# A fused attention and rational feed-forward kernel: the engines' order written by hand, elementwise work in one piece a block, K turned by DMA

## The chip, the cores and the metric

One core of one Trainium2 chip. The metric is device time in microseconds (us) of one execution; lower is better. The kernel before has a median of 319.29 us (315.65 to 320.66, 4 runs). Medians and ranges in this document are over all runs; ratios use the fast ones alone (a run more than 1.5% above the fastest of its kernel counts as slow, as 320.66 does).

The engines go by short names: PE multiplies matrices, DVE (VectorE), ACT (ScalarE) and POOL (GpSimd) work element by element; SP and POOL also issue DMA transfers (copies to and from the chip's memories), which land some us later. SBUF is the on-chip memory, PSUM the banks into which PE writes. To "turn" is to transpose; the "spread" copies the turned K into the layout that the scores need.

## The reference, cut to what matters

```python
# attention: 4 batches, 8 heads, 768 positions, head dimension 64
scores = q @ k.T / sqrt(64)
keep   = (column < 4) | ((row - column >= 0) & (row - column < 128))   # 4 sinks and a window of 128
a      = softmax(where(keep, scores, -1e9));   x = a @ v               # x: 3072 x 512
# feed-forward: 512 -> 2048 -> 512, the activation is a quotient of two polynomials
h = x @ w_in
P = a0 + a1*h + a2*h**2 + a3*h**3
Q = 1 + |b0|*|h| + |b1|*h**2
out = (P / (Q + 1e-6)) @ w_out                                          # float32
```

The 3072 tokens are worked in 12 blocks of 256 (three to a batch). A block is 256 tokens times 2048 features; on chip that is 128 partitions times 4096 elements.

## The kernel before: the parts that matter

Both kernels divide h by |b0|/|b1| so that Q needs no coefficients: x or w_in is multiplied by one scalar, `csc`. The quotient is num * exp(-ln(Q)): DVE does the polynomial in bf16, ACT the logarithm and the exponential. The elementwise functions work on **half** a block:

```python
UC = NFFC // 2;  UW = UC * TS                      # 2048 elements a partition: half a block
# ... cut ...
def load_w_in(half):                               # w_in scaled on its way to bf16
    for c in range(NDMC):
        nc.sync.dma_start(out=t_f, in_=moe_w_in[...])
        nc.vector.tensor_scalar(out=w_in_sb[c][:, f0:f1], in0=t_f, scalar1=csc, scalar2=None, op0=ALU.mult)
# ... cut ...
def turn_k(s):                                     # K: 8 transposes on PE, then spread out of PSUM
    ps = ps_mp.tile([P, 512], FP32, tag="ps_m", name="ps_kT").bitcast(BF16)
    for t in range(NTS):
        for i in range(NPB):
            nc.tensor.transpose(ps[:, i, t * P:(t + 1) * P], kb[:, t, i * P:(i + 1) * P], ident)
    for e in range(2):
        nc.vector.tensor_copy(out=kT[lo:hi, :, lo:hi], in_=ps[lo:hi]...)
# ... cut: scores, exps, mask, attend ...
        nc.vector.tensor_tensor(out=dst, in0=o4[...], in1=rec[...], op=ALU.mult)      # x normalised
# ... cut ...
def even(i):       nc.vector.tensor_scalar(out=num[i], in0=sq[i], scalar1=a2, scalar2=a0, ...)
def odd(i):        nc.vector.tensor_scalar(out=sq[i], in0=sq[i], scalar1=a3, scalar2=a1, ...)
def odd_h(i):      nc.vector.tensor_tensor(out=sq[i], in0=sq[i], in1=hb[i], op=ALU.mult)
def numerator(i):  nc.vector.tensor_tensor(out=num[i], in0=num[i], in1=sq[i], op=ALU.add)
def gate(i):       nc.vector.tensor_tensor(out=g_of[m, u], in0=num[i], in1=den[i], op=ALU.mult)
# ... cut ...
for i in range(-3, NU + 4):                        # one half block a turn; scores three half blocks ahead
    # scores(i + 3), attend(i + 2), project_in(i), elementwise(i, i - 1), project_out(i - 3)
```

The program order of this loop is only a proposal: the framework's scheduler decides in which order each engine gets its instructions.

The softmax here doesn't subtract the row's maximum and nothing guards it: scores larger than these inputs give would overflow.

## Time and profile before

| | before |
|---|---|
| median us | 319.29 |
| first 256-token block at w_in (first `ps_h` matmul) | 44.31 us |
| third block at w_in (the milestone of the prediction) | 102.25 us |
| pace from the fourth block's `even` to the eighth's | 20.52 us a block |
| DVE busy, 200 to 220 us | 19.30 of 20 us |

The milestone is the first product that needs the second half of the third block's x; a few matmuls on its first half come before (at 92.20 us here). The pace is read from the starts of the DVE operation `even` (of its first half here): 136.81 us in the fourth block and 218.89 in the eighth. These four blocks have the whole list of work in every kernel; behind them the spreads of K run out, in some kernels one block earlier than in others. (The prediction took 19.85 from later blocks and another row; by `even` these, from 198.78 to 278.22 us, give 19.86.)

### The profile page before, as it was taken

The numbers are of one execution on the slowest core, as the hardware profiler recorded it, in microseconds if no ns is written. First come the engines' busy times: TensorE is split into PE (matmuls) and PEld (weight loads), VectorE is DVE, ScalarE is ACT, GpSimd is POOL, SyncE is SP. The second block draws the span as 40 slices with busy tenths as digits, with TensorE's granted clock in tenths as the row PEclk, the third lists the DMA queues.
The fourth block names the chain that finished last, engine by engine and source line by source line (L and its number), as shares of the span: only waits on it lengthen the run. The fifth ranks groups of instructions, "written<-read, shape, count | busy, mean of one in ns | idle before, by whom it ended". The sixth has DMA issues, their size and how long they took to land.

```text
span 318.6 us, 5033 instructions
## 1 busy us (share of the span) xinstructions
PE 240.5 (75%) x1920; PEld 167.4 (53%) x1920; DVE 250.4 (79%) x384; ACT 212.8 (67%) x194; POOL 127.1 (40%) x192
## 2 busy tenths in 40 slices
PE   0025448749348969998879989989899898979964
PEld 0014336638224746666647665577575675746521
DVE  7534520769936897899998999999999899897990
ACT  1013014657823993996878978889799897877951
POOL 9986667996884341534540113356200000000000
PEclk9999556979858998999999999999999999999999
DMA  4999999999999996996960627549510111110011
GB/s 132 111 209 192 204 184 151 99 131 103 111 107 136 102 123 84 86 82 86 107 76 17 76 54 56 72 58 107 72 44 22 36 51 49 35 33 33 35 66 66
DMA packets 110775, 28.67 MB, mean 90 GB/s; under 512 B 104608, under 2 KB 106656, under 8 KB 110752
## 3 DMA queue, kind: packets, MB, share of 16 engines
q0 software_dynamic: 78976, 11.56, 58.1%
q1 hardware_dynamic: 31776, 16.79, 23.6%
q8 instruction: 15, 0.25, 0.3%
q14 instruction: 8, 0.07, 0.1%
HBM read 27.30 MB, written 6.29 MB: 105 GB/s over the span
## 4 chain that ended last, share of the span: by engine, by line
DVE 33%; ACT 21%; DMA 19%; PE 10%; issue 7%; POOL 5%; SPq 3%; DVEq 0%; ACTq 0%; POOLq 0%
DMA xblk<-x_n 12%; ACT lnq L379 7%; ACT den L383 6%; DVE den L358 5%; DVE g L388 5%; PE ps_h L339 5%; DVE num L373 4%; DVE sq L370 4%; PE ps_out L398 3%; ACT e L274 3%; SPq L324 3%; DVE den L354 3%; ACT hb L342 3%; DVE num L362 2%; DMA q_bf<-in_q_dram 2%
## 5 line engine op out<-in xcount | busy, mean ns | idle before, releaser
L339 PE MATMUL ps_h<-xblk,w_in_sb 128*128 128x256 bf16 x768 | 98.0, 278 | 30.7 <-DMA xblk<-x_n 30.6
L339 PEld LDWEIGHTS <-w_in_sb 128*128 128x128 bf16 x768 | 74.4, 100 | 45.6 <-DMA xblk<-x_n 28.1
L398 PE MATMUL ps_out<-w_out_sb,g 128*128 128x512 bf16 x384 | 93.5, 391 | 3.7 <-DVE g L388 3.4
L97 POOL DMA_DIRECT2D v_bd<-in_v_dram x96 | 61.8, 663 | 55.4 <-PE ps_o L305 47.3
L274 ACT ACTIVATE e<-ps_s 128x768 bf16<-128x768 f32 x48 | 38.7, 806 | 53.2 <-PE ps_s L270 53.2
L342 ACT ACTIVATE hb<-ps_h 128x1024 bf16<-128x1024 f32 x48 | 48.7, 1018 | 21.1 <-PE ps_h L339 21.1
L398 PEld LDWEIGHTS <-g 128*128 128x128 bf16 x384 | 37.3, 101 | 44.0 <-issue 5.1
L379 ACT ACTIVATE lnq<-den,one_eps,qsc 128x2048 f32<-128x2048 bf16 x24 | 50.2, 2092 | 5.5 <-DVE den L358 5.5
L383 ACT ACTIVATE den<-lnq 128x2048 bf16<-128x2048 f32 x24 | 45.8, 1908 | 0.0
L270 PE MATMUL ps_s<-qT,kT 128*128 128x192 bf16 x192 | 27.4, 272 | 9.4 <-DVE kT L237 7.3
L305 PE MATMUL ps_o<-v_bd,e 128*128 128x130 bf16 x352 | 31.4, 226 | 3.0 <-DMA v_bd<-in_v_dram 1.8
L388 DVE TENSOR_TENSOR g<-num,den 128x2048 bf16<-128x2048 bf16 x24 | 29.4, 1223 | 5.4 <-ACT den L383 5.3
L358 DVE TENSOR_TENSOR den<-den,sq 128x2048 bf16<-128x2048 bf16 x24 | 29.4, 1223 | 2.5 <-ACT sq L348 2.0
L281 DVE TENSOR_TENSOR e<-e,edge 128x1024 bf16<-128x1024 bf16 x24 | 16.2, 675 | 17.7 <-ACT e L274 17.7
L373 DVE TENSOR_TENSOR num<-num,sq 128x2048 bf16<-128x2048 bf16 x24 | 29.3, 1222 | 0.4
L370 DVE TENSOR_TENSOR sq<-sq,hb 128x2048 bf16<-128x2048 bf16 x24 | 29.1, 1214 | 0.1
L305 PEld LDWEIGHTS <-e 128*128 128x128 bf16 x352 | 26.1, 101 | 5.2 <-issue 3.5
L88 POOL DMA_DIRECT2D k_bf<-in_k_dram x24 | 22.2, 931 | 15.9 <-PE ps_kT L232 14.9
L80 POOL DMA_DIRECT2D q_bf<-in_q_dram x24 | 21.7, 906 | 17.2 <-DMA qT<-q_bf 17.2
L270 PEld LDWEIGHTS <-kT 128*128 128x128 bf16 x192 | 18.0, 108 | 16.4 <-DVE kT L237 9.8
L348 ACT ACTIVATE sq<-hb 128x2048 bf16<-128x2048 bf16 x12 | 22.9, 1911 | 0.3
L232 PE MATMUL ps_kT<-ident,k_bf 128*128 128x128 bf16 x96 | 8.1, 233 | 19.9 <-POOL ident masks.py:199 18.9
(56 smaller groups left out, 224.1 us busy)
## 6 DMA issues: line engine op xcount, KB each, us to landing
out_dram<-o_t SPq DMA_DIRECT2D x24, 256.0 KB, 2.1
w_in_f<-in_moe_w_in_dram SPq DMA_DIRECT2D x8, 512.0 KB, 5.8
q_bf<-in_q_dram POOLq DMA_DIRECT2D x24, 128.0 KB, 4.8
k_bf<-in_k_dram POOLq DMA_DIRECT2D x24, 128.0 KB, 4.8
v_bd<-in_v_dram POOLq DMA_DIRECT2D x96, 32.0 KB, 3.8
w_out_sb<-in_moe_w_out_dram POOLq DMA_DIRECT2D x16, 128.0 KB, 6.7
xblk<-x_n SPq DMA_TRANSPOSE x48, 2.5
qT<-q_bf SPq DMA_TRANSPOSE x24, 4.0
```

The source lines that it names most:

```text
L97: nc.gpsimd.dma_start(out=t_[e * 64:(e + 1) * 64, i, :, e, 0:D], in_=v[b, h, g * TS:(g + 1) * TS, :].rearrange("(j p) d -> p j d", p=64))
L270: nc.tensor.matmul(ps[:, n // 2, (n % 2) * 192:(n % 2) * 192 + 192], lhsT=kT_fix[s % 2][:, i * NHF + n, :], rhs=qT_fix[b % 2][:, i, c:c + ...
L274: nc.scalar.activation(out=data.rearrange("p (a n) c -> p a n c", a=2), in_=ps[:, :, 0:384].rearrange("p a (n c) -> p a n c", n=2), func=A ...
L305: nc.tensor.matmul(ps_o[:, n, :], lhsT=l_, rhs=r_.rearrange("p e c -> p (e c)"), start=(m == 0), stop=(m == len(terms) - 1))
L339: nc.tensor.matmul(ps_h[:, n, :], lhsT=w_in_sb[c][:, fc * P:(fc + 1) * P], rhs=xblk[m][:, c, :], start=(c == 0), stop=(c == NDMC - 1))
L342: nc.scalar.activation(out=hb[i][:, half * w:(half + 1) * w], in_=ps_h.rearrange("p n c -> p (n c)"), func=AF.Copy)
L358: nc.vector.tensor_tensor(out=den[i], in0=den[i], in1=sq[i], op=ALU.add)
L373: nc.vector.tensor_tensor(out=num[i], in0=num[i], in1=sq[i], op=ALU.add)
L379: nc.scalar.activation(out=lnq[i], in_=den[i], func=AF.Ln, scale=qsc, bias=one_eps)
L383: nc.scalar.activation(out=den[i], in_=lnq[i], func=AF.Exp, scale=-1.0)
L388: nc.vector.tensor_tensor(out=g_of[m, u], in0=num[i], in1=den[i], op=ALU.mult)
L398: nc.tensor.matmul(ps_out[m, tt], lhsT=g_of[m, u][:, co:co + P], rhs=w_out_sb[fc], start=(fc == 0), stop=(fc == NFFC - 1))
```

## The change

The intent: keep DVE, the bound, without holes and give it less to do. `manual_schedule` turns the scheduler off, so that every engine works in program order; the loop goes over quarter blocks ("slots"), with the scores two blocks (eight slots) ahead of their block's w_in product, and w_out ten slots behind. Five elementwise kinds take a whole block at once (4096 wide). K is turned by DMA transposes on SP from the third block on. The first loads go raw through SP, and the first two blocks' K, Q and x are turned on PE. The scalar `csc` moves from w_in to the normalisation of x. PSUM changes too: a pool of two banks shared by four users becomes one bank for scores of sinks and attention, and one for w_out.

The diff has 938 lines; this is its core, with cuts marked:

```diff
+    ctx.enter_context(tc.manual_schedule())
...
-    ps_mp = ctx.enter_context(tc.tile_pool(name="ps_m", bufs=2, space=bass.MemoryType.PSUM))
+    ps_mp = ctx.enter_context(tc.tile_pool(name="ps_m", bufs=1, space=bass.MemoryType.PSUM))
+    ps_op = ctx.enter_context(tc.tile_pool(name="ps_o", bufs=1, space=bass.MemoryType.PSUM))
...
+    load_k(0)                                     # raw, on SP
+    for n in range(NQ_HW):
+        load_q(n)
+    load_v(0)
     nc.sync.dma_start(out=b_bc, in_=moe_b.partition_broadcast(P))
...
+        kT_flat[s] = a_kv.tile([P, NPB, TS], BF16, tag="kT_flat", name="kT_flat", bufs=3)
+        for t in range(NTS):
+            nc.sync.dma_start_transpose(out=kT_flat[s][:, :, t * P:(t + 1) * P], in_=kb[:, t, :])
...
-        nc.vector.tensor_tensor(
+        nc.vector.scalar_tensor_tensor(
+            out=dst, in0=o4[:, :, 0:D].rearrange("p (n e) c -> p n e c", e=2), scalar=csc,
...
+    ahead_s = {0: (), 1: (4, 5), 2: (6, 7), 3: (), 4: (8, 9), 5: (10, 11), 6: (12, 13),
+               7: (14, 15)}
+    ahead_a = {0: (), 1: (), 2: (4, 5), 3: (6, 7), 4: (), 5: (8, 9), 6: (10, 11), 7: (12, 13)}
+    spread_at = {4: 2, 6: 3, 7: 4}
+    turn_at = {0: 2, 2: 3, 4: 4, 6: 5}
+    for t in range(NSLOT + 14):
+        p, j = divmod(t, 4)
+        ns = ahead_s.get(t, (t + 8,))             # scores of this slot
+        na = ahead_a.get(t, (t + 6,))             # attends of this slot
...
+        if s < NSTEP:
+            turn_qk(s)
+            if s != 3:
+                feed(s + 2)
+        if t in (4, 5):
+            load_w_out(t - 4)
+        if t == 5:
+            feed(5)
...
+            if in_g:
+                gate(c - 1)                       # 4096 wide, as even, odd, odd_h, numerator
```

## The prediction

> **What bounds the kernel now.** I read the page first: the DVE row and the DMA row of its slices.
>
> ```profile
> PE 240.5 (75%) x1920; PEld 167.4 (53%) x1920; DVE 250.4 (79%) x384; ACT 212.8 (67%) x194; POOL 127.1 (40%) x192
> DVE  7534520769936897899998999999999899897990
> DMA  4999999999999996996960627549510111110011
> ```
>
> No engine is full on average, but the average mixes two stages: until about 110 us the DMA is full and DVE is not; after it, DVE is at 9 and the DMA falls away. The table of busy time by stretch, for one early and one late stretch, gives both (columns: stretch, its length, then busy us with counts of PE, weight load, DVE, ACT, POOL; clock, DMA share, GB/s):
>
> ```profile
> 80.00:100.00 20.00, 9.94 (x63) 5.55 (x60) 12.56 (x23) 9.65 (x10) 16.45 (x23) 0.66 1.86 110
> 200.00:220.00 20.00, 18.62 (x164) 13.35 (x162) 19.30 (x31) 17.69 (x17) 9.47 (x14) 1.00 0.66 64
> ```
>
> Late, DVE is busy 19.3 of 20 us: it is the bound. Early, every compute engine waits. The chain of waits says for what:
>
> ```profile
> 86.41 5.75 DMA xblk<-x_n
> 92.20 1.03 PE ps_h L339 x4
> 98.10 4.10 DMA xblk<-x_n
> 102.25 1.72 PE ps_h L339 x14
> 310.98 3.64 PE ps_out L398 x16
> ```
>
> The turned x block is asked for one half step before its use, and under the load of the early DMA it takes 4 to 7 us to land. The third 256-token block reaches w_in at 102.25 us; I use that point as a milestone. The ACT timeline gives the late pace, one lnq per half block:
>
> ```profile
> 198.92 2.08 ACT L379 ACTIVATE lnq<-den,one_eps,qsc 128x2048 f32<-128x2048 bf16 x1
> 278.34 2.10 ACT L379 ACTIVATE lnq<-den,one_eps,qsc 128x2048 f32<-128x2048 bf16 x1 [0.81 <-DVE den L358]
> ```
>
> Eight half blocks in 79.4 us: **19.85 us a block**, 12 blocks in all. So the time is 102 us to the milestone, then 216 us for ten blocks and the drain.
>
> **What the Trainium skill says.** (1) "VectorE: DVE Perf Modes", section "Side-by-side: where the cycles go for N=2048 bf16": 2048 elements cost about 1224 ns at two per cycle, of which some 150 cycles are fixed. The trace agrees for the two-input operations (1223, below), so a 4096-wide one is estimated at (2048+150)/0.96 = 2.29 us. The one-input ones read 0.82 here, not the page's 0.69 (they carry two per-partition scalars); I keep the trace's fixed part, 0.82 - 0.53 = 0.29, and estimate 1.07 + 0.29 = 1.36 us at 4096. (2) The same page, "Why PSUM operands drop a tier": a copy out of PSUM cannot run four per cycle. The K spread out of PSUM takes 684 ns for 1024 elements; out of SBUF I estimate (256+150)/0.96 = 0.42 us. (3) "TensorE: Matmul & The Clock Gate", section "Wait — 56ns, not 53.3ns?": a warm matmul starts every N/2.4 + 2.5 ns; sixteen of 512 then take 3.45 us, and the chain's last line has 3.64 with the end of the last, which agrees. (4) "DMA: Bandwidth & Descriptors", section "Issuing engines are not separate DMA queues": loads moved to another issuer still share the 16 engines. The early stretch, with both queues in use and xblk slow, agrees.
>
> ```profile
> L358 DVE TENSOR_TENSOR den<-den,sq 128x2048 bf16<-128x2048 bf16 x24 | 29.4, 1223 | 2.5 <-ACT sq L348 2.0
> L362 DVE TENSOR_SCALAR num<-sq,acoef 128x2048 bf16<-128x2048 bf16 x24 | 19.6, 815 | 0.1
> L237 DVE COPY kT<-ps_kT 64x1024 bf16<-64x1024 bf16 x24 | 16.4, 684 | 0.2
> L313 DVE TENSOR_TENSOR x_n<-ps_o,rec 128x256 bf16<-128x256 f32 x48 | 20.0, 418 | 0.1
> ```
>
> **The change part by part, in the steady stage, per block.** Neighbouring DVE operations overlap by about 0.09 us in the timeline, so I count from start to start.
> - Five of nine elementwise kinds go from 2x2048 to 1x4096. Three two-input ones: 6 x 1.17 = 7.0 becomes 3 x 2.25 = 6.75. Two one-input ones: 4 x 0.84 = 3.4 becomes 2 x 1.37 = 2.75. Saved 0.9.
> - K turned by DMA: two copies of 0.69 become two of about 0.39, and the k_sink copies go from 16 to 4 in the whole kernel. Saved 0.6 + 0.2. PE loses eight transposes (0.45 us).
> - x scaled at the normalisation: 48 operations get a scalar operand (I give 0.05 each, four per block, 0.2 lost); the eight w_in scalings (6.0 us in all) leave DVE, at the start only.
> - The list for a block: normalise 2.5, mask 1.2, magnitude 1.2, square 1.1, denominator 2.3, even and odd 2.75, odd_h and numerator 4.5, gate 2.2, spread 0.9 = 18.6. The same list for before gives 19.6 against 19.15 observed busy, so scaled by 0.977 it is 18.2.
> - PE by columns: 41,400 per block / 2.4 + 147 x 2.5 ns = 17.6 us. ACT from its group means, start to start: 4 x 0.92 + 4 x 0.72 + 2 x 2.0 + 2 x 1.82 + 1.82 + 2 x 0.5 + 0.3 = 17.3 us.
> Three engines within 5%; with 0.5 us lost to one another I take **18.7 us a block**, 1.15 below 19.85.
>
> **The start.** The first block's K, Q, V go raw through SP from 0.8 us (before, Q left POOL at 6.8 us behind 5.4 us of memsets) and are turned on PE, as are the first two x blocks, in place of the 7.1 us xblk wait. I expect the first ps_h at about 25 us instead of 44.3. But the loads cannot keep up: before, POOL issued a block of k, q, v in about 10 us (0.93, 0.91 and 0.66 us an issue) and the 16 w_out took 14 us (32 to 46 us). In the new program order SP has the turn of K and Q of block 5 **ahead of** the second half of xblk of block 2, and POOL has the load of that K and Q **behind** all of w_out. POOL's clock, with those issue times, at most eight loads outstanding (before, it also stops behind its own earlier loads) and landings of 4.5 to 8 us: v_sink issued by 9 us; w_in's first half and k, q of block 1 by 15; v 1 behind the landing of w_in, 17 to 22; w_in's second half and k, q 2 by 28; v 2 behind its landing, 30 to 36; k, q 3 by 39, k, q 4 behind the turned K of block 2 by 43; v 3 by 48; k, q 6 by 52; w_out from 52, of which the ninth has to land before k of block 5 goes, at 66. It lands at 73, its q at 75; four turns of 1.2 us on SP, then xblk, 2.4 to 4 us to landing: **83 us** for the milestone that was 102. On compute alone it would be there at about 61.
>
> **The drain.** Blocks 2 to 9: 8 x 18.7 = 150. Block 10 has no scores and half the attends (15.8), block 11 neither (14.5). Then DVE has one block of elementwise work and two gates, 15.8; PE four times eight matmuls, 7.0; and 4.2 from the last matmul to the end (before: 314.6 to 318.6). The pipeline is longer, so this drain of 27 us is longer than before's 21.6. Some 3 us of block 1's DVE work is done during the wait before block 2. Sum: 83 + 150 + 15.8 + 14.5 + 27 - 3 = **287**; I say 288.
>
> **Rivals.**
> - A: no stall before block 2. If the loads run faster than I added, the milestone is near 61 to 65 us and the time 268 to 272. For it: the leads look tuned, and the saturated DMA did move 1127 packets per us for 5 us (50 to 55 us). Against: POOL's issue times alone, up to that load, sum to 57 us.
> - B: the single ps_s buffer and the single ps_m and ps_out banks replace the wait. Scores of a slot wait for the exps of the one before, and ACT's slots are uneven (a 1.8 us Square lies between two of them), so PE, ACT and DVE take turns waiting; then a block stays at 19.8 and the time is about 297 to 300. For it: before, ACT waited 53.2 us for ps_s. Against: most of that is the start, and the uneven slots leave PE more than 1 us.
> - C: turning K through the DMA (20 more transposes, 1.2 us each on SP) saturates SP or the DMA, and xblk comes late in the steady stage as it did early. Then 305 to 320. Against: SP would be busy 8 x 1.23 + 2 x 0.33 = 10.5 of 18.7 us, the DMA's late share is 0.66.
>
> **Range and chances.** My sum has two uncertain terms: the milestone, 83 with 10 either way, and ten blocks at 18.7 with 0.6 either way, so 6. Together about 12; rival A is more likely than C. Range 272 to 303. Slower or same needs C, or both B and a late milestone: 6%.
>
> **What would show it.** Right: first ps_h near 25 us; PE idle 10 to 25 us on xblk once, between 60 and 85 us, with SP at that time waiting for k_bf or q_bf; later 18.3 to 19.2 us per block with DVE above 95%; a 4096-wide two-input operation at 2.29 us and a one-input one at 1.36; the spread at about 0.42. Wrong: no such wait (A), a pace of 19.5 or more with idle DVE behind ps_o or e (B), repeated xblk waits after 120 us (C).

## More of the kernel before

In the chain of work that ended last DVE is only a third, since until 110 us the chain runs over ACT and DMA:

```profile
DVE 33%; ACT 21%; DMA 19%; PE 10%; issue 7%; POOL 5%; SPq 3%; DVEq 0%; ACTq 0%; POOLq 0%
```

## The result, and the profile after

Ratios in this document are the mean time of one kernel's fast runs over that of the other's of the same rounds, so not quite the ratio of the medians that are quoted. The changed kernel has a median of **297.51 us** (297.16 to 298.49, 4 runs), a ratio of 0.936 (95% interval 0.928 to 0.944): faster, 9.5 us above the predicted 288 and inside the range.

The page of the changed kernel: counts of DVE instructions fell from 384 to 320, DVE's row is at 9 from 100 us on, the DMA row stays high until about 200 us (before: about 165), and the chain that ended last now runs over DVE for more than half of the span.

```profile
PE 235.5 (79%) x1856; PEld 167.4 (56%) x1876; DVE 239.3 (81%) x320; ACT 214.2 (72%) x201; POOL 116.1 (39%) x178
DVE  6606623736794999999999999999999999999930
DMA  8999999999999199398995999292110121100111
DVE 56%; PE 16%; DMA 8%; ACT 7%; issue 6%; SPq 5%; POOL 1%; DVEq 0%; ACTq 0%; POOLq 0%
```

The table of busy time by stretch (columns as in the prediction) has the two stages, as before:

```profile
80.00:100.00 20.00, 10.25 (x87) 8.37 (x87) 15.22 (x19) 11.70 (x11) 8.64 (x12) 0.74 0.98 74
200.00:220.00 20.00, 18.98 (x162) 13.98 (x162) 19.78 (x23) 18.60 (x18) 0.00 (x0) 1.00 0.20 47
```

Late, DVE is busy 19.78 of 20 us instead of 19.30. The groups that changed, with the mean ns of one:

```profile
L474 DVE TENSOR_TENSOR num<-num,sq 128x4096 bf16<-128x4096 bf16 x12 | 27.5, 2292 | 0.4
L384 DVE SCALAR_TENSOR_TENSOR x_n<-ps_o,csc,rec 128x256 bf16<-128x256 f32 x48 | 23.2, 484 | 1.7
L460 DVE TENSOR_SCALAR num<-sq,acoef 128x4096 bf16<-128x4096 bf16 x12 | 16.1, 1344 | 0.2
L293 DVE COPY kT<-kT_flat 64x1024 bf16<-64x1024 bf16 x20 | 8.4, 418 | 0.1
```

These answer to 1222 (num, half a block), 418 (x_n), 815 (even, half a block) and 684 (spread) of before. In the start, the matmul that waits is the milestone: PE's timeline shows it held for 7.54 us.

```profile
81.25 0.38 PE L419 MATMUL ps_h<-xblk,w_in_sb 128*128 128x256 bf16 x2
89.18 3.17 PE L419 MATMUL ps_h<-xblk,w_in_sb 128*128 128x256 bf16 x14 [7.54 <-DMA xblk<-x_n]
```

The time of the profiled run, cut at the milestone (PE timeline; blocks counted from 1), next to before's:

| | before | after |
|---|---|---|
| start to block 3 | 102.25 | 89.18 |
| block 3 to the end | 216.35 | 207.62 |
| span | 318.6 | 296.8 |

So 13.1 us come from the start and 8.7 from the rest. No run takes the start's gain apart (raw loads on SP, turns on PE, order), nor the new PSUM banks.

The end, in the chain of waits: after the last gate the two output tiles of the last block take turns in one PSUM bank, and PE stands still between them while ACT empties it.

```profile
282.62 2.30 DVE g L492
284.97 3.64 PE ps_out L500 x16
288.69 0.61 ACT o_t L505
289.33 3.63 PE ps_out L500 x16
293.03 0.60 ACT o_t L505
```

### The profile page after: what moved, and what is told of

It reads as the page before. It is cut to its first block, busy times and chain, and to the rows that moved or that the text cites. A ratio compares the mean times of both kernels' runs of the same rounds, so it can differ in the third digit from the quotient of the medians.

```text
span 296.8 us, 4876 instructions
## 1 busy us (share of the span) xinstructions
PE 235.5 (79%) x1856; PEld 167.4 (56%) x1876; DVE 239.3 (81%) x320; ACT 214.2 (72%) x201; POOL 116.1 (39%) x178
## 4 chain that ended last, share of the span: by engine, by line
DVE 56%; PE 16%; DMA 8%; ACT 7%; issue 6%; SPq 5%; POOL 1%; DVEq 0%; ACTq 0%; POOLq 0%
DVE sq L470 8%; DVE num L474 8%; PE ps_h L419 7%; DVE g L492 6%; DVE den L454 6%; DVE x_n L384 5%; DVE num L460 4%; DVE den L449 4%; DVE e L348 4%; PE ps_out L500 4%; DVE sq L443 3%; PE ps_o L371 3%; DMA b_bc<-in_moe_b_dram 3%; DVE sq L465 2%; ACT hb L426 2%
## 5 line engine op out<-in xcount | busy, mean ns | idle before, releaser
L500 PE MATMUL ps_out<-w_out_sb,g 128*128 128x512 bf16 x364 | 87.8, 385 | 7.6 <-ACT o_t L505 4.0
L419 PEld LDWEIGHTS <-w_in_sb 128*128 128x128 bf16 x768 | 76.4, 102 | 20.5 <-DMA xblk<-x_n 7.8
L151 POOL DMA_DIRECT2D v_bd<-in_v_dram x88 | 57.3, 670 | 28.7 <-PE ps_o L371 12.2
L131 POOL DMA_DIRECT2D k_bf<-in_k_dram x22 | 20.3, 937 | 46.9 <-DMA kT_flat<-k_bf 46.6
L331 PE MATMUL ps_s<-qT,kT 128*128 128x192 bf16 x192 | 25.7, 260 | 14.9 <-ACT e L341 14.6
L331 PEld LDWEIGHTS <-kT 128*128 128x128 bf16 x192 | 18.4, 104 | 17.7 <-issue 16.2
L474 DVE TENSOR_TENSOR num<-num,sq 128x4096 bf16<-128x4096 bf16 x12 | 27.5, 2292 | 0.4
L492 DVE TENSOR_TENSOR g<-num,den 128x4096 bf16<-128x4096 bf16 x12 | 27.4, 2284 | 0.1
L470 DVE TENSOR_TENSOR sq<-sq,hb 128x4096 bf16<-128x4096 bf16 x12 | 27.4, 2284 | 0.1
L384 DVE SCALAR_TENSOR_TENSOR x_n<-ps_o,csc,rec 128x256 bf16<-128x256 f32 x48 | 23.2, 484 | 1.7
L381 DVE RECIPROCAL rec<-ps_o 128x4 f32<-128x4 f32 x48 | 8.5, 177 | 18.7 <-PE ps_o L371 18.5
```

Source lines behind the costliest of these rows:

```text
L151: nc.gpsimd.dma_start(out=t_[lo:hi, i, :, e, 0:D], in_=src)
L331: nc.tensor.matmul(ps[:, n // 2, (n % 2) * 192:(n % 2) * 192 + 192], lhsT=kT_fix[s % 2][:, i * NHF + n, :], rhs=qT_fix[b % 2][:, i, c:c + ...
L419: nc.tensor.matmul(ps[:, n, :], lhsT=w_in_sb[c][:, fc * P:(fc + 1) * P], rhs=xblk[m][:, c, :], start=(c == 0), stop=(c == NDMC - 1))
L470: nc.vector.tensor_tensor(out=sq[m][:, c], in0=sq[m][:, c], in1=hb[m][:, c], op=ALU.mult)
L474: nc.vector.tensor_tensor(out=num[m][:, c], in0=num[m][:, c], in1=sq[m][:, c], op=ALU.add)
L492: nc.vector.tensor_tensor(out=g_of[m][:, c], in0=num[m][:, c], in1=den[m][:, c], op=ALU.mult)
```

## The experiments

Twelve kernels ran, in four groups, each group on one chip and timed in turn with the kernel before. Each is the changed kernel with one edit, unless said. "Pace" is the mean of four blocks, from `even` of the fourth to that of the eighth block in DVE's timeline; in the first profile of the changed kernel it is 18.74. (The block behind these would make it unfair: it has no spread of K except in e10_k_pe_later and in the kernel before.)

| run | edit | median us (range, runs) | ratio to before | pace us |
|---|---|---|---|---|
| after_again | none | 298.11 (297.18 to 299.47, 4) | 0.934 | 18.83 |
| e1_sched | scheduler on | 314.70 (313.69 to 315.61, 4) | 0.985 | 18.31 |
| e3_narrow | five kinds in halves | 301.30 (301.12 to 301.95, 4) | 0.944 | 19.18 |
| e4_k_pe | K on PE | 310.01 (309.41 to 310.57, 4) | 0.971 | 20.39 |
| e5_b_first | b, a first on SP | 299.18 (297.37 to 299.69, 6) | 0.936 | 18.74 |
| e6_feed5 | K, Q of block 6 before w_out | 297.02 (295.48 to 297.48, 7) | 0.930 | 18.57 |
| e7_sp | their turn behind the x block | 294.76 (293.72 to 298.45, 6) | 0.923 | 18.67 |
| e8_tail | split drain | 294.77 (294.53 to 295.49, 6) | 0.923 | 18.74 |
| e9_all | e5 to e8, last gate in quarters | 288.27 (287.36 to 288.74, 6) | 0.904 | 18.65 |
| e10_k_pe_later | K on PE, spread one operation later | 302.27 (300.34 to 305.40, 6) | 0.947 | 19.30 |
| e11_w_scaled | csc on w_in again | 298.12 (296.41 to 298.77, 6) | 0.934 | 18.42 |
| e12_best | e9 and csc on w_in, placed in waits | 288.44 (286.86 to 289.67, 6) | 0.903 | 18.46 |

The code counts blocks from 0: its "block 2" and "block 5" in the prediction and in the expectations are the third and the sixth. One run of e7_sp (298.45) and one of e10_k_pe_later (305.40) were slow; without them the medians are 294.38 and 302.14. e1 to e4 and the unedited run share a chip with e5 to e8; the rest ran on two others, whose kernel before had medians of 318.62 and 321.22 us. A thirteenth kernel, the one before with `manual_schedule`, did not build: in program order its engines wait for each other in a ring (it stops with a deadlock), so the hand-written order could not be tried alone on the old loop.

### The changed kernel again

> The changed kernel once more, unedited, on the chip of the next three runs, so that they have it beside them: 297.5 us as before, ratio to the kernel before 0.936. Anything beyond 1.5 us from that would be the chip's own spread.

298.11 us: the chip repeats it within 0.6 us. Its chain of waits happens to run straight through the wait ahead of block 3, piece by piece, as the prediction told it: POOL's load of the sixth block's K behind w_out, its landing, four turns on SP, then the x block's own turn.

```profile
71.28 5.34 DMA k_bf<-in_k_dram
76.64 1.66 SPq L284
78.40 1.21 SPq L284
79.70 1.22 SPq L265
81.01 1.22 SPq L265
82.32 1.20 SPq L407
83.57 6.17 DMA xblk<-x_n
89.79 2.31 PE ps_h L419 x10
```

### The order given back to the scheduler

> The changed kernel without its hand-written order: one line less, and the framework's own scheduler places the instructions of every engine. Theory: the order is what shortens the start and keeps the DVE list without holes; the wide operations then only save 0.9 us a block, so the time goes back to 305 to 325 us. Rival: the wide operations, the K by DMA and the start through PE carry the gain (fewer, cheaper instructions), and the order is an incidental: 295 to 302 us.

```diff
-    ctx.enter_context(tc.manual_schedule())
```

314.70 us, 16.6 us slower than the changed kernel: the theory's range, and the rival (the order is incidental) falls. But the theory's reason is half wrong. In the four blocks the **pace is not worse** without the hand-written order, 18.31 us against 18.83 (with 15 normalisations in the stretch instead of 16). There the scheduler sets other operations between odd_h and the numerator, which depend on one another, and odd_h takes 2.20 us from start to next start instead of 2.31. The loss is at both ends. `even` of the fourth block starts at 145.77 instead of 137.88 us, 7.9 later; that of the ninth at 236.50 instead of 230.97, 5.5 later; that of the last at 286.16 instead of 276.10, 10.1 later; and the span ends at 312.4 instead of 297.8, 14.6 later. In the start the first w_in product comes 9 us **earlier** (21.88 us), but PE then waits for x blocks five times, 19.8 us in all (changed kernel: once, 7.5 and 9.2 in its two profiles). From the ninth `even` to the last it takes 49.7 us against 45.1, so that over all eight blocks from the fourth it is 2.2 us slower. So what the order buys is a start without repeated waits on x, and short last blocks and drain; in the middle it costs half a us a block.

### Width

> The five 4096-wide kinds as two 2048-wide halves each, same place in the order. Theory (width step of the prediction): 0.9 us of DVE a block, DVE the bound from about 100 us on, so ten to eleven blocks give +9 to +10 us: about 307 us. Rival: the narrower operations let ACT and PE start on a half sooner, which gives back most of it: +0 to +4 us. DVE's pace, even to even, should go from 18.5 to 19.4 us.

```diff
-                gate(c - 1)
+                gate(c - 1, A_)
+                gate(c - 1, B_)
...                 # the same for even, odd, odd_h, numerator
```

301.30 us, +3.2 on the same chip, where the theory said +9 to +10. The rival's figure holds (+0 to +4), but not its reason: ACT and PE wait for nothing less. The pace rises by only 0.35 us, so the width itself is worth that little. The DVE timeline says why. First the changed kernel, then the narrow one; the first column is the start:

```profile
193.71 1.36 DVE L460 TENSOR_SCALAR num<-sq,acoef 128x4096 bf16<-128x4096 bf16 x1
194.99 0.72 DVE L449 TENSOR_SCALAR den<-hb 128x1024 uint32<-128x1024 uint32 x1
...
197.49 2.28 DVE L470 TENSOR_TENSOR sq<-sq,hb 128x4096 bf16<-128x4096 bf16 x1
199.80 2.29 DVE L474 TENSOR_TENSOR num<-num,sq 128x4096 bf16<-128x4096 bf16 x1
```

```profile
195.75 1.54 DVE L460 TENSOR_SCALAR num<-sq,acoef 128x2048 bf16<-128x2048 bf16 x2
197.21 0.72 DVE L449 TENSOR_SCALAR den<-hb 128x1024 uint32<-128x1024 uint32 x1
...
199.89 2.35 DVE L470 TENSOR_TENSOR sq<-sq,hb 128x2048 bf16<-128x2048 bf16 x2
202.16 2.35 DVE L474 TENSOR_TENSOR num<-num,sq 128x2048 bf16<-128x2048 bf16 x2
```

From start to next start, `even` takes 1.28 us wide and 1.46 as two halves: 0.18 saved. But odd_h takes 2.31 wide and 2.27 as halves: nothing saved. Two halves are independent, and the second starts before the record of the first ends: each costs about 1.13 us, not the 1.22 of its record. The wide numerator needs the wide odd_h before it and doesn't start early (2.31 us behind it, for a record of 2.28), so there nothing is left to save. Over the five kinds I read 0.18 + 0.19 - 0.04 + 0.06 + 0 = 0.39 us a block, close to the pace's 0.35.

### K on PE, twice

> K turned on PE in every block (eight transposes and a spread out of PSUM), no K transposes on SP. Theory (DVE bound): two spreads of 686 ns in place of 418 add 0.54 us a block, and PE's transposes wait for the single ps_m bank, +0.5 us more at most: 4 to 10 us slower in the blocks, and up to 5 us won back at the stall before block 2, where SP no longer waits for k_bf: 297 to 305 us in all. Rival (SP and DMA are what is short): faster than the changed kernel by 3 us or more, 285 to 294.

```diff
-        if s < NS_PE:
+        if True:                                  # turn_k: always on PE
...
     def spread_k(s):
+        if s >= NS_PE:
+            turn_k(s)
...                 # cut: k_bf gets a third buffer; the early turns and the DMA transposes of K go
```

310.01 us, +11.9: past the theory's 297 to 305, in its direction; the rival (faster) falls. The pace is 1.56 us longer, of which the longer spread (two of 686 instead of 418 ns) explains 0.54. The rest is the handing over: DVE stands still for 0.9 us a block while PE turns K, and later in the same block PE stands still behind DVE, which is late with the mask (0.75) and with x_n, whose PSUM bank the sinks' scores need (1.16). One block's timeline (DVE, then PE):

```profile
201.27 1.39 DVE L292 COPY kT<-ps_kT 64x1024 bf16<-64x1024 bf16 x2 [0.90 <-PE ps_kT L278]
212.45 0.52 PE L370 MATMUL ps_o<-v_bd,e 128*128 128x130 bf16 x6 [0.75 <-DVE e L347]
```

> K turned on PE in every block as in the run before, but the spread out of PSUM goes behind DVE's next operation (even), so that DVE does not stand still for the transposes. Theory: of the 1.8 us a block that K on PE cost, 0.54 was the longer spread and the rest the handing over through the single bank; with the handing over hidden, DVE's pace is 19.1 us a block and the time 302 to 304. Rival: PE's own wait for the bank (attends behind the spread) is the cost, and moving the spread back makes it longer: 308 us or more.

```diff
                 log_den(c, B_)
                 even(c)
+            if ahead < NSTEP:
+                spread_k(ahead)                   # instead of ahead of even
```

(On top of the edit of the run before.) 302.27 us, in the theory's 302 to 304; DVE no longer waits for `ps_kT` in the steady blocks, and the pace is 19.30, 0.47 above the changed kernel's. So K by DMA is worth about 0.5 us a block for what it is: the cheaper copy (0.54) explains all of it. It is worth 1.56 us where the PE version hands over badly. The rival is out: the spread moved back made the kernel 7.7 us faster (7.4 by the two ratios, since the chips differ), not slower.

### The wait ahead of block 3, and the first block

> Only the order of SP's first DMAs: the small coefficients go ahead of K, Q and V instead of behind them. Theory (start): the first ps_h comes at 25 to 27 us instead of 31.1, since ACT no longer waits for b in order. At the end: if the stall before block 2 is bound by the loads (POOL and SP, which do not move), 0 to 2 us faster; rival, if the first two blocks set it by compute, 5 to 6 us faster.

```diff
+    nc.sync.dma_start(out=b_bc, in_=moe_b.partition_broadcast(P))
+    nc.sync.dma_start(out=a_bc, in_=moe_a.partition_broadcast(P))
     load_k(0)
```

299.18 us: no gain, as the theory said for the end. In the changed kernel the chain to the first w_in product runs over the landing of two coefficients, issued behind eight loads of V:

```profile
12.22 9.29 DMA b_bc<-in_moe_b_dram
```

With them first, the product comes at 28.98 us, 1.7 us earlier than in the unedited run (30.63) and not at 25 to 27: DVE now waits for V itself, which was due hardly earlier.

```profile
DVE v_bd L156 <- DMA stage_kv<-in_v_dram: 5.1, 1, 5.1
```

And the third block still comes at 89.72 us (unedited: 89.79); PE's wait for it grew from 9.24 to 10.79 us. A wait that ends on a load eats what is gained ahead of it.

> K and Q of block 5 are loaded ahead of w_out instead of behind it. Theory: SP's turn of block 5 no longer waits for k_bf (last landed behind w_out), the second half of the x block goes on time, and the 7.5 us PE wait before block 2 goes to under 3: 4 to 7 us faster, 291 to 294. Rival: w_out comes 4 us later and its first use waits, or the DMA is just full, so the x block lands late anyway: within 2 us.

```diff
-            if s != 3:
+            if s != 4:
                 feed(s + 2)
...
-            feed(5)
+            feed(6)
```

297.02 us, 1.1 less: the rival's "within 2". SP waits less for k_bf (3.0 us between 40 and 100 us, 8.9 in the first profile of the changed kernel) and issues the x block's second half 5 us earlier, at 77.4. But that half now takes 8.12 us to land instead of 5.53:

```profile
78.64 8.12 DMA xblk<-x_n
```

It was issued right behind the loads of w_out and of the next K and Q, which POOL sent between 62 and 77 us; that these are what slowed it is likely but was not shown apart (in the next run, with POOL issuing no loads beside it, it lands in 2.3 us). PE still waits 6.0 us, and the third block comes at 86.81 us.

> SP's turn of K and Q of block 5 is put one step later, behind the second half of the x block of block 2; the loads stay where they are. Theory: the wait is one of order on SP only, so the 7.5 us PE wait before block 2 goes to under 3 us and the end comes 4 to 7 us earlier, 291 to 294. Rival: the x block lands late because the DMA engines are full, or the turn of block 5 comes late for its scores: within 2 us.

```diff
-    turn_at = {0: 2, 2: 3, 4: 4, 6: 5}
+    turn_at = {0: 2, 2: 3, 4: 4, 7: 5}
```

294.76 us, 3.3 less, against 4 to 7 expected. The wait is gone; of PE's idle time ahead of w_in only the first blocks' remains:

```profile
L419 PE MATMUL ps_h<-xblk,w_in_sb 128*128 128x256 bf16 x768 | 99.8, 287 | 0.7 <-ACT xblk L404 0.7
```

The third block comes at 84.53 us, 5.3 earlier than in the unedited run, but at 84.53 **without any wait**: the computation of the first two blocks is not ready before. (PE's granted clock was lower in this profile, 0.59 to 0.82 between 20 and 80 us against 0.91 to 1.00; in the unedited run PE was there at 80.17.) This profiled run, 296.73 us, is the slowest of the five fast ones. The edit also does more than the expectation says: `feed` hangs on the turn, so POOL sends the eighth block's K and Q at 86.73 us instead of 81.70, and the x block, issued 2.5 us earlier, lands in 2.3 us instead of 4.3 to 5.5. So the wait was the order on SP, together with the loads beside the x block (how much each was not tried apart), and close behind it stood compute. Of the 5.3 us the end keeps 3.3: `even` of the second block starts only 2.1 us earlier (98.55 against 100.62), because DVE did elementwise work during the wait that it now does after it.

### The drain

> The drain alone: the last two blocks' elementwise work and gates in halves, and the halves of w_out accumulated in two PSUM banks, so that half the matmuls run beside DVE's last operations. Theory: after the last gate 14 us pass now, of which 7.3 are 32 matmuls behind it and 4 are waits for the one bank; half of the matmuls and the wait go: 4 to 6 us faster, 291 to 294; narrower operations cost 0.9 of it. Rival: DVE's list with narrow operations becomes longer by what PE saves: within 2 us.

```diff
-    for t in range(NSLOT + 14):
+    for t in range(NSLOT):
...
+    for h in (A_, B_):                            # the last block, half by half
+        even(y, h)
+        odd(y, h)
+        odd_h(y, h)
+        numerator(y, h)
+        gate(y, h)
+        if h is A_:
+            ...
+            project_out(y, 0, 0, 8, ps_mp)        # its own bank
+            project_out(y, 1, 0, 8)
+    project_out(y, 0, 8, 16)
+    project_out(y, 1, 8, 16)
```

294.77 us, 3.3 less; expected were 4 to 6. Sixteen matmuls are left behind the last gate instead of 32, and no wait for a bank between them:

```profile
284.29 1.24 DVE g L492
285.57 3.64 PE ps_out L500 x16
```

The narrow last operations cost some of it: here each depends on the one before, so nothing overlaps (odd_h starts at 281.69, the numerator at 282.95, 1.26 later).

### All of these together, and the scaling of x

> Together: coefficients first on SP, K and Q of block 5 loaded ahead of w_out, their turn behind the x block on SP, and the split drain, whose last gate now goes in two quarters. Alone they gave 0, 1, 3.3 and 3.3 us. Theory (after the stall DVE is the bound, so only what shortens DVE's list before its first full block or behind its last counts): the stall is worth 3 once, the drain 3.3 and the quarters 1.2, sum 7.5, so 290 us (288.5 to 291.5). Rival: with no stall the earlier first ps_h counts too, as does every us of the early wait: 6 us more, 283 to 286.

288.27 us, ratio 0.904 to the kernel before: **better than both kernels**. It lies 0.2 below the theory's range and 2 above the rival's; the parts' single gains (0, 1.1, 3.3, 3.3) and an estimated 1.2 for the quartered gate sum to 8.9, and 298.1 to 288.3 is 9.8 (on two chips; by the two ratios it is 9.5). The third block comes at 82.92 us, and PE waits for it still:

```profile
82.92 3.17 PE L419 MATMUL ps_h<-xblk,w_in_sb 128*128 128x256 bf16 x14 [3.59 <-DMA xblk<-x_n]
```

> The scaling of x in the normalisation undone: w_in is scaled in place, in eight DVE operations in the first 45 us, and the normalisation is a plain product of two tensors again. Theory (DVE bound from 100 us on): 484 goes to 418 ns, four times a block, 0.26 us a block, so 2.5 to 3 us over the ten blocks in which DVE is the bound, and the eight added operations lie where DVE is idle half of the time: 294.5 to 296 us. Rival: the added operations delay the first blocks by 3 to 4 us and the gain is lost: 297 to 299.

```diff
-        nc.vector.scalar_tensor_tensor(
-            ..., scalar=csc, in1=rec..., op0=ALU.mult, op1=ALU.mult)
+        nc.vector.tensor_tensor(..., in1=rec..., op=ALU.mult)
...
+    scale_w_in(0)                                 # 4 operations in place, behind the first two x columns
...
+        if t == 0:
+            scale_w_in(1)
```

298.12 us: no gain, the rival. The pace did fall by 0.41 us, to 18.42; four x_n of 425 instead of 484 ns explain 0.24 of it. But the first w_in product came 1.4 us later than in the unedited run (32.03), and `even` of the second block 1.2 us later; what the blocks win is then gone again in the sum.

> The combined kernel (288.3 us) with the scaling moved from x to w_in once more, but with the eight added operations placed where DVE waits: the first four while it waits for V to land (4.7 us idle there), the others two and two around the turn of Q. Theory: the run that scaled w_in gained 0.15 to 0.28 us a block later and lost it again because its first four operations stood in front of the first x block; without that loss 1.5 to 3 us remain: 285.5 to 287. Rival: the gain is none, since PE and ACT, busy 19.2 and 18.8 of 20 us, become the bound as soon as DVE is shorter: 288 to 289.

288.44 us, the same as without it (288.27; ratios 0.903 and 0.904). Placed in waits, the added operations no longer delay the first product (28.24 us), but the second half's do delay the third slice (39.87 against 38.14 us in e9_all). The pace was 18.46 against 18.65: a little over 1 us in seven blocks (128.4 against 129.7 us from the second block to the ninth), which the start takes back. Where csc is applied is a wash. The expected rival (PE and ACT become the bound) is not what happened: DVE stayed at 19.5 to 19.7 of 20 us.

## Why the prediction was right or wrong

The range held, and in the main the mechanism; the figure was 9.5 us low. Its sum, term by term, against the profiled run (296.8):

| term | predicted | measured |
|---|---|---|
| start to the third block (milestone) | 83 | 89.2 |
| eight blocks at the pace | 150 (18.7 each) | 148.1 |
| less the work done during the wait | -3 | in the row above: the first of the eight took 17.3, so 1.4 |
| the last two blocks | 15.8 + 14.5 | 15.0 + 14.2 |
| drain | 27 | 30.3 |
| sum | 287 | 296.8 |

(The rows after the first are read from the starts of w_in products of the third, fourth, eleventh and twelfth block: 89.18, 106.47, 237.31, 252.34 us, and 266.5 where the next would have come.)

- **The first w_in product, "near 25 us": wrong, 31.10.** The prediction added up K, Q and x and forgot that two tiny loads stand behind V on the same queue. Moving them gave 1.7 us and then V was the wait; and none of it counted, since the third block waits for other loads.
- **The milestone, 83: right mechanism, 6 us short.** The predicted chain is there link by link (the unedited run's chain). Its terms: POOL issued the sixth block's K at 70.40 instead of 66; four turns on SP took 5.5 to 6.0 us instead of 4.8; the x block took 5.5 to 6.2 us to land instead of 2.4 to 4 (2.3 is what it takes without loads beside it, in e7_sp). The last was the worst choice: the prediction had 4 to 7 us under load in front of it, in the profile of before, and took less.
- **"PE idle 10 to 25 us" and "on compute alone ... about 61": wrong.** The wait was 7.5 us because PE was not there before 81.25 us. The first two blocks took 50 us (31.1 to 81.25), not 36. The lists `ahead_s` and `ahead_a` in the diff are the likely reason, which no edit tried, and should have been counted: in those eight slots twelve scores and ten attends are done, not eight each, to build up the lead; and PE's clock was granted at 0.83 to 0.91 in 40 to 80 us. No engine was full there (busy per 20 us: PE 13 to 14, ACT 10 to 14, DVE 9 to 11): PE waited 8.0 us for exponentials, ACT 15.2 us for w_in products and DVE 11.5 us for attends, which is the taking turns of rival B, in the start. e7_sp shows the limit: with the wait gone the third block comes at 84.53 (at the lower clock of that profile; in the changed kernel's own two PE was there at 80.2 and 81.3). Rival A ("no stall", 268 to 272) was therefore never possible. The two errors, a late load and a late computation, hid each other: that the milestone came within 6 us of the forecast is in part luck.
- **The pace, 18.7: right to 0.1 us (18.74 and 18.83), by a sum whose terms were not.** The width was to save 0.9 us and saves 0.35 to 0.4 (e3_narrow). The step that failed is "Three two-input ones: 6 x 1.17 = 7.0 becomes 3 x 2.25 = 6.75. Two one-input ones: 4 x 0.84 = 3.4 becomes 2 x 1.37 = 2.75": the durations of single operations were right (2292 and 1344 ns, predicted 2.29 and 1.36), but not their starts: two narrow ones behind each other take 2.27 and 1.46. A page that I did not use has the better figure: the Trainium skill, "Vector Engine (DVE) Microarchitecture Reference", section "5.2 Measured stream behaviour on trn2 (trn3 not measured)", gives about 75 ns a DVE instruction beyond its columns once the queue overlaps them. Five instructions fewer a block are then, as an estimate, 0.38 us, and the runs agree: 0.35 by the pace, 0.39 by the starts.
- **K by DMA, "0.6 + 0.2": the first term a little high.** 0.47 by e10_k_pe_later; e4_k_pe shows that it can be three times that where PE and DVE take turns at one bank. The 0.2 for the k_sink copies was not tried apart (their busy time goes from 1.9 to 0.8 us in the whole kernel, 0.1 a block).
- **x scaling, 0.2 lost: 0.41 by e11_w_scaled, 0.19 by e12_best against e9_all**, and the start gives it back.
- **What makes 20.52 into 18.83** (the same four blocks) is settled in part. Of the 1.69 us a block, 0.69 are fewer holes (DVE idle 0.96 us a block before, 0.27 after) and 1.00 is less busy time. Of that the tried parts give 0.35 + 0.47 less 0.19 to 0.41, so 0.4 to 0.6; the rest, about 0.5, was not isolated. The hand-written order is not needed for it, since with the scheduler the pace was 18.31.
- **The drain, 27: 3.3 us short.** The prediction counted one block's elementwise work and two gates, 15.8; DVE had 18.4 us to do there, the numerator of the block before included (2.3). Behind the last gate come 32 matmuls, with 0.73 us of waiting for the one output bank between them (the 4 us in the expectation of e8_tail are such waits over the whole drain). The prediction's "4.2 from the last matmul to the end" is 4.0 by its own two figures; after, it is 3.9.
- **Rival B** (single banks take turns, 19.8 us a block) did not hold in the steady stage: DVE was busy 19.78 of 20 us. One reading was loose: "until about 110 us the DMA is full" is true, but its row falls away only from about 165 us. **Rival C** fell with e4_k_pe and with the absence of x waits after 100 us.

## What to carry to other kernels

When a change builds up a lead, count what the first turns do: they carry the lead's work as well, and a wait at their end may be hidden behind it or hide it. Read the worth of merging elementwise operations from start to start in the timeline, and ask whether neighbours depend on one another: independent ones already overlap, and merged ones that form a chain don't. An order written by hand pays where queues meet (which load stands ahead of which turn, which bank is shared in the drain) and not where one engine is full anyway; after the big change, four small moves of that kind gave 3% more.

## What the Trainium skill lacked or had wrong

- "VectorE: DVE Perf Modes", section "The DRAIN you can't avoid", says that after every DVE operation the next one does not start until the pipe is empty, and that one that is not held starts earlier; it has no number for the difference. The runs have: independent 2048-wide products start 1.13 us apart at a recorded 1.22 us each, which the 75 ns cited above also give, as an estimate; dependent ones start 1.26 us apart, for which I found none.
- I found no page that gives durations for operations with per-partition scalars apart: a 2048-wide one-input operation in bf16 with two of them takes 815 to 824 ns, a 4096-wide one 1339 to 1344; one scalar with two tensors, one of them in PSUM, takes 484 ns where the plain product takes 418 to 425 (128x256).
- I found no page that says how long a DMA transpose takes beside loads: the third block's x landed 5.0 to 8.1 us after its issue in e5_b_first, e6_feed5, e9_all and the changed kernel, and 2.3 us after it in e7_sp, where POOL issued no loads meanwhile. SP is occupied for 1.2 us at each issue.
